# Loading each value row once, and copying the shared half tile on GpSimd, for the first four token tiles of a fused attention and two-MoE kernel

## The chip, the cores and the metric

The kernel runs on one core of one Trainium2 chip. Its time is the device time of one execution in microseconds (us). A core has five engines with an instruction queue each: PE (TensorE, matrix products), DVE (VectorE), ACT (ScalarE), POOL (GpSimd) and SP (SyncE, which here only starts transfers). The engines run side by side and wait for one another through semaphores; each takes its own instructions strictly in the order in which they stand. Transfers (DMA) from the chip's memory are cut into packets, which 16 DMA engines share.

## What is computed

Sliding-window attention over 4 sequences of 576 tokens with 8 heads of 64 values, then two feed-forward layers over all 2304 tokens. All inputs are f32.

```python
def _attn_ref(q, k, v):                     # (4, 8, 576, 64) each
    scores = scale * np.matmul(q, k.transpose(0, 1, 3, 2))
    mask = (rel >= 0) & (rel < window)      # rel = row - column, window = 64
    ...
    return np.matmul(attn, v)
...
h = x @ w_in                                # 512 x 2048
g = np.where(pos, h, np.where(neg, 0.0, (h + beta) ** 2 / (4.0 * beta)))
x = g @ w_out                               # 2048 x 512
...                                         # second layer: 512 x 1024, soft-max gate, layer norm, 1024 x 512
```

With a window of 64, a query looks at the 64 rows of its own range and at the 64 rows of the range ahead of it, and at no others.

## The kernel before

**Tiles.** Tokens go in 12 tiles of 192 (TT), three to a sequence. A tile has three ranges of 64 queries (QB). For each range i of tile t the kernel holds one value tile `vw[t, i]` of 128 rows by 8 heads by 64: rows 0 to 63 are the value rows of the preceding range, rows 64 to 127 those of the range itself. So the lower half of one value tile holds the same rows as the upper half of the one before it. `load_v(t)` (L294 to L303) fills the three tiles of t by three transfers from SP, each of 256 KB, in a ring of 6 buffers. For the first range of a sequence, which has nothing ahead of it, it loads only 64 rows, its own (128 KB), into the lower half, and the products there use 64 rows only (`first`, L341).

**Attention.** A group g is one tile and one pair of heads (4 groups to a tile). `st_qkt` puts queries and keys into shape, `st_s` makes the scores (PE into ps_s at L352, DVE L360 for mask and maximum, ACT L366 for the exponentials), `st_norm` divides by the sum (DVE L377 and L378, then L382 and L386 on POOL for the first three tiles and on DVE afterwards), `st_t` transposes the weights on PE (ps_p, L400 and L402, brought back by ACT L405 and L407), and `st_v` multiplies with the value tiles (ps_x, L421) and splits the result into a high and a low part (ACT L428 to xh, DVE L429 to xl).

**First layer.** Tokens go in 6 blocks of 384 (j). For each of 16 slices f of the hidden width, `moe_h` makes ps_h (L496, 12 matmuls), the gate is formed on ACT, DVE and POOL (L505, L506, u at L511, gh at L512, gl at L516; L516 is on POOL in block 0 and on DVE later), and `moe_y` adds into four accumulators (L527, 12 matmuls). In block 0 the slices f = 0 and 1 are done in two halves: first for the tokens of tile 0, then for those of tile 1. The numbers U0, U1, ... below count the L511 instructions: U0 and U1 are the two slices of tile 0, U2 and U3 those of tile 1, U4 is f = 2 for all 384 tokens.

**Weights.** The first layer's weights are loaded during block 0 and kept. Each of 32 units W0 to W31 (512 KB each, two for each slice f, alternating w_in and w_out) passes one conveyor: a transfer by SP into one of 5 staging buffers wst (L124 or L126), DVE L136, ACT L132, DVE L137, ACT L145 (the high part, wih or woh), POOL L146 (the low part, wil or wol). Only when POOL is through with a unit is its staging buffer free for the transfer of the unit five places later.

**What sets the order.** The source issues work in slots, but a scheduler orders each engine's instructions from the time it supposes that each takes. A change in one transfer therefore moves instructions on all engines. After block 0, PE goes through blocks 1 to 5 and the second layer.

## Time and profile before

| | us |
|---|---|
| median of 3 runs (lowest to highest) | 710.56 (709.49 to 712.19) |
| profiled execution | 712.67 |
| its span, first to last instruction | 710.9 |
| PE busy in the span | 685.6 |
| block 0, about | 0 to 130 |
| PE busy from 0 to 130 | 112.7 |
| PE busy from 130 to 432 (302 us) | 302.0 |

The profile counts from the first instruction; 1.8 us of the profiled execution lie around its span. A stretch is read by asking what the engine that sets the pace waited for in it. PE is busy without a break from 130 to 432, so of the first layer it is block 0 that holds PE's idle time. The granted TensorE clock is given as a share of 2.4 GHz, so 0.50 is the lower of its two levels, 1.2 GHz.

### The profile page before, as it was taken

To read this page: it belongs to the slowest core of one execution; us is meant where nothing else is said; L and a number is where in the kernel's file an instruction comes from. 1 tells how busy PE (TensorE), PEld (TensorE's weight loads), DVE (VectorE), ACT (ScalarE), POOL (GpSimd) and SP (SyncE) were. 2 spreads that over 40 slices of the span, in tenths; PEclk is the share of its full clock that TensorE was granted. 3 is DMA by queue.
4 is the path that set the end of the run, shared out by engine and by line. 5 is a ranking of instruction groups with operands and counts; after the bars stand their busy time and mean duration, and the time that the engine had idled before them with its cause. 6 is when DMAs were issued, how large, how long until landed. Compare 5 with 4: busy or idle time off the path is not lost.

```text
span 710.9 us, 12663 instructions
## 1 busy us (share of the span) xinstructions
PE 685.6 (96%) x4439; PEld 630.0 (89%) x4439; DVE 434.3 (61%) x1147; ACT 413.0 (58%) x1006; POOL 195.3 (27%) x217
## 2 busy tenths in 40 slices
PE   6899978999999999999999999999999899999998
PEld 5689768999999999999999999999988678888887
DVE  4549898555555555454455543642379799988850
ACT  5778886565566655565566665454455635545541
POOL 2358876200001000021112111652472223300000
PEclk9989999999999999999999999999999999999999
DMA  9986897534353623346352211452033554553321
GB/s 193 216 231 171 220 260 189 107 81 107 71 110 88 139 61 73 78 124 130 87 112 70 95 60 47 154 200 89 1 126 97 175 164 155 175 177 122 131 74 45
DMA packets 155544, 88.94 MB, mean 125 GB/s; under 512 B 118616, under 2 KB 141400, under 8 KB 155480
## 3 DMA queue, kind: packets, MB, share of 16 engines
q1 hardware_dynamic: 144040, 64.00, 36.4%
q0 software_dynamic: 8704, 19.41, 8.4%
q10 hardware_dynamic: 2736, 4.72, 1.8%
q8 instruction: 35, 0.57, 0.4%
q14 instruction: 29, 0.24, 0.1%
HBM read 63.97 MB, written 24.12 MB: 124 GB/s over the span
## 4 chain that ended last, share of the span: by engine, by line
PE 72%; DVE 10%; issue 7%; POOL 4%; DMA 3%; ACT 2%; SPq 1%; DVEq 0%; POOLq 0%; ACTq 0%
PE ps_h L496 22%; PE acc L527 22%; PE ps_o L826 13%; PE P L711 7%; PE ps_x L476 2%; PE ps_p L402 2%; PE ps_s L442 2%; PE ps_s L352 2%; DVE wst L137 2%; POOL wil L249 2%; DVE wst L136 1%; PE ps_x L421 1%; DMA wst<-in_moe_w_out_dram 1%; DVE gl L516 1%; DVE s L740 1%
## 5 line engine op out<-in xcount | busy, mean ns | idle before, releaser
L511 DVE SCALAR_TENSOR_TENSOR u<-u,ps_h 128x384 f32<-128x384 f32 (+1 forms) x98 | 53.2, 543 | 143.8 <-ACT u L506 140.2
L496 PE MATMUL ps_h<-xh,wih 128*128 128x384 f32 (+1 forms) x392 | 132.6, 339 | 3.2 <-DVE u L511 3.1
L496 PE MATMUL ps_h<-xl,wih 128*128 128x384 f32 (+1 forms) x392 | 131.5, 336 | 1.4 <-DVE xl L429 1.4
L527 PE MATMUL acc<-gl,woh 128*128 128x384 f32 (+1 forms) x392 | 130.7, 335 | 2.2 <-DVE gl L516 1.3
L496 PE MATMUL ps_h<-xh,wil 128*128 128x384 f32 (+1 forms) x392 | 131.5, 336 | 0.0
L527 PE MATMUL acc<-gh,wol 128*128 128x384 f32 (+1 forms) x392 | 129.7, 333 | 0.0
L527 PE MATMUL acc<-gh,woh 128*128 128x384 f32 (+1 forms) x392 | 126.9, 342 | 0.0
L505 ACT ACTIVATE u<-ps_h,half 128x384 f32<-128x384 f32 (+1 forms) x98 | 55.9, 572 | 92.6 <-PE ps_h L496 92.4
L512 ACT CAST gh<-u 128x384 fp32r<-128x384 f32 (+1 forms) x98 | 49.7, 507 | 55.0 <-DVE u L511 37.8
L496 PEld LDWEIGHTS ps_h<-xh,wih 128*128 128x128 f32 x392 | 74.6, 190 | 5.2 <-DVE u L511 4.7
L527 PEld LDWEIGHTS acc<-gl,woh 128*128 128x128 f32 x392 | 73.8, 188 | 3.5 <-DVE gl L516 1.7
L496 PEld LDWEIGHTS ps_h<-xl,wih 128*128 128x128 f32 x392 | 74.7, 190 | 2.2 <-DVE xl L429 2.0
L516 DVE TENSOR_TENSOR gl<-u,gh 128x384 fp32r<-128x384 f32 x80 | 52.8, 661 | 37.3 <-ACT gh L512 36.7
L527 PEld LDWEIGHTS acc<-gh,woh 128*128 128x128 f32 x392 | 72.4, 188 | 3.0 <-issue 2.4
L496 PEld LDWEIGHTS ps_h<-xh,wil 128*128 128x128 f32 x392 | 74.7, 190 | 0.1
L527 PEld LDWEIGHTS acc<-gh,wol 128*128 128x128 f32 x392 | 73.7, 188 | 0.0
L711 PE MATMUL P<-wih,x2p 128*128 128x512 f32 x216 | 70.6, 391 | 0.5 <-DVE xo L539 0.5
L826 PE MATMUL ps_o<-woh,wol 128*128 128x512 f32 (+1 forms) x152 | 58.6, 385 | 2.9 <-DVE wol L814 2.9
L826 PE MATMUL ps_o<-woh,woh 128*128 128x512 f32 (+1 forms) x152 | 58.4, 384 | 0.0
L826 PE MATMUL ps_o<-wol,woh 128*128 128x512 f32 (+1 forms) x152 | 58.0, 382 | 0.0
L506 ACT ACTIVATE u<-u 128x384 f32<-128x384 f32 (+1 forms) x98 | 51.0, 521 | 2.0
L711 PEld LDWEIGHTS P<-wih,x2p 128*128 128x128 f32 x216 | 40.5, 188 | 9.2 <-DVE xo L539 0.9
(125 smaller groups left out, 1250.8 us busy)
## 6 DMA issues: line engine op xcount, KB each, us to landing
vw<-in_v_dram SPq DMA_DIRECT2D x32, 256.0 KB, 5.2
wst<-in_moe_w_in_dram SPq DMA_DIRECT2D x16, 512.0 KB, 5.2
wst<-in_moe_w_out_dram SPq DMA_DIRECT2D x16, 512.0 KB, 5.5
lnd<-e SPq DMA_DIRECT2D x16, 512.0 KB, 2.7
lT<-lnd SPq DMA_DIRECT2D x64, 128.0 KB, 3.0
x2d<-xo POOLq DMA_DIRECT2D x24, 192.0 KB, 2.5
out_dram<-o ACTq DMA_DIRECT2D x17, 256.0 KB, 2.9
wst<-in_moe_w_in_dram POOLq DMA_DIRECT2D x8, 512.0 KB, 5.3
```

Of the source, the lines that this page charges most:

```text
L137: nc.vector.scalar_tensor_tensor(high, high, 3, low, op0=ALU.logical_shift_left, op1=ALU.bitwise_or)
L249: nc.gpsimd.tensor_tensor(lo, v_, as_f32(hi), op=ALU.subtract)
L352: nc.tensor.matmul(ps[:, i * 128 + c0:i * 128 + 128], qT[g][:, i, :, :].rearrange("p x q -> p (x q)"), kT[g][:, i * 64 + c0:i * 64 + 128], ...
L496: nc.tensor.matmul(ps, a, bb[:, kc, c], start=(n == 0), stop=(n == 3 * KC - 1))
L505: nc.scalar.activation(u, ps, ACTF.Relu, bias=half, scale=0.5)
L506: nc.scalar.activation(u, u, ACTF.Square)
L511: g = nc.vector.scalar_tensor_tensor(u, u, 1.0, ps, op0=ALU.min, op1=ALU.max)
L512: return nc.scalar.copy(hi, u).ins, g.ins
L516: eng.tensor_tensor(lo, u, as_f32(hi), op=ALU.subtract)
L527: nc.tensor.matmul(acc[j, e][:, c], a, bb, start=(f == 0 and n == 0 and c.start == 0), stop=(f == NF - 1 and n == 2),)
L711: nc.tensor.matmul(ps, l, r, start=(n == 0), stop=(n == 5))
L826: nc.tensor.matmul(ps, a[kk // 4][:, kk % 4, :], b[kk][:, c:c + w], start=(n == 0), stop=(n == 3 * NK2 - 1),)
```

## The change

For tiles t = 0 to 3 (NVC = 4), `load_v` loads only the 64 rows of the range itself, into the upper half of the value tile (128 KB), and GpSimd copies the upper half of the preceding value tile into the lower half. The first range of a sequence no longer has a tile of its own: it uses the lower half of the second range's tile, which is still loaded whole (`vw[t, 0] = vw[t, 1]`). From tile 4 on nothing is changed.

```diff
-    G0, F0, NC, NQ, NV = 6, 2, 4, 6, 7
+    G0, F0, NC, NQ, NV, NVC = 6, 2, 4, 6, 7, 4
...
         for i in range(QB):
-            w = at_p.tile([128, H, D], F32, tag="vw", bufs=6, name="vw")
             s0 = tl * TT + i * 64 - 64
+            if t < NVC and s0 < 0:
+                continue
+            w = vw[t, i] = at_p.tile([128, H, D], F32, tag="vw", bufs=6, name="vw")
             if s0 < 0:
                 nc.sync.dma_start(out=w[0:64], in_=v[b, :, 0:64, :].rearrange("h p d -> p h d"))
+            elif t < NVC and s0 > 0:
+                nc.sync.dma_start(out=w[64:128], in_=v[b, :, s0 + 64:s0 + 128, :].rearrange("h p d -> p h d"))
+                nc.gpsimd.tensor_copy(w[0:64], (vw[t, i - 1] if i else vw[t - 1, QB - 1])[64:128])
             else:
                 nc.sync.dma_start(out=w, in_=v[b, :, s0:s0 + 128, :].rearrange("h p d -> p h d"))
-            vw[t, i] = w
+        if t < NVC and tl == 0:
+            vw[t, 0] = vw[t, 1]
```

Lines behind L304 stand 6 further down in the changed kernel (L386 is L392 there, and so on). The copies are L305. There are 8 of them: one for tile 0, three each for tiles 1 and 2, one for tile 3; they are called C0 to C7 below.

**POOL, from the start to the normalization of group 2.** The names are p (softmax weights of a group), rs (reciprocal sums) and vw (value tiles). Before:

```order
L382 TENSOR_TENSOR p<-p,rs 128x64
L386 TENSOR_TENSOR p<-p,rs 128x256
L382 TENSOR_TENSOR p<-p,rs 128x64
L386 TENSOR_TENSOR p<-p,rs 128x256
L382 TENSOR_TENSOR p<-p,rs 128x64
```

Now, at the same place:

```order
L305 COPY vw<-vw 64x512
L388 TENSOR_TENSOR p<-p,rs 128x64
L392 TENSOR_TENSOR p<-p,rs 128x256
L305 COPY vw<-vw 64x512
L388 TENSOR_TENSOR p<-p,rs 128x64
L392 TENSOR_TENSOR p<-p,rs 128x256
L146 TENSOR_TENSOR wil_146<-wst,wih_145 128x512
```

C0 stands ahead of the first group's normalization and C1 ahead of the second's; W0's low part has moved ahead of group 2.

**PE, around the weight transposes of group 6 (the last ps_p here).** wih_168 and wil_169 before, and wih_170 and wil_171 now, are the two parts of unit W2, of the slice f = 1. Before:

```order
L402 MATMUL ps_p<-ident,p 128x128 x3
L421 MATMUL ps_x<-pT,vw 64x64 x6
L402 MATMUL ps_p<-ident,p 128x128 x3
L496 MATMUL ps_h<-xh,wih_168 128x192
L496 MATMUL ps_h<-xl,wih_168 128x192
```

Now:

```order
L502 MATMUL ps_h<-xl,wih_170 128x192
L502 MATMUL ps_h<-xh,wil_171 128x192
L502 MATMUL ps_h<-xh,wih_170 128x192
L502 MATMUL ps_h<-xl,wih_170 128x192
L502 MATMUL ps_h<-xh,wil_171 128x192
L427 MATMUL ps_x<-pT,vw 64x64 x7
L408 MATMUL ps_p<-ident,p 128x128 x3
L427 MATMUL ps_x<-pT,vw 64x64 x5
```

All of slice f = 1 for tile 0 now stands ahead of group 6's transposes; before, it stood behind them.

**POOL, from unit W4 (wil_177 before, wil_179 now) on.** Before:

```order
L146 TENSOR_TENSOR wil_177<-wst,wih_176 128x512
L516 TENSOR_TENSOR gl<-u,gh 128x192
L386 TENSOR_TENSOR p<-p,rs 128x384
L516 TENSOR_TENSOR gl<-u,gh 128x192
L146 TENSOR_TENSOR wol_364<-wst,woh_363 128x512
L146 TENSOR_TENSOR wil_412<-wst,wih_411 128x512
L386 TENSOR_TENSOR p<-p,rs 128x384
L516 TENSOR_TENSOR gl<-u,gh 128x192
L386 TENSOR_TENSOR p<-p,rs 128x384
L516 TENSOR_TENSOR gl<-u,gh 128x192
L146 TENSOR_TENSOR wol_461<-wst,woh_460 128x512
```

Now, from the second copy of tile 2 (C6) to U2's gl:

```order
L305 COPY vw<-vw 64x512
L146 TENSOR_TENSOR wil_414<-wst,wih_413 128x512
L392 TENSOR_TENSOR p<-p,rs 128x384
L146 TENSOR_TENSOR wol_463<-wst,woh_462 128x512
L146 TENSOR_TENSOR wil_500<-wst,wih_499 128x512
L146 TENSOR_TENSOR wol_524<-wst,woh_523 128x512
L392 TENSOR_TENSOR p<-p,rs 128x384
L146 TENSOR_TENSOR wil_533<-wst,wih_532 128x512
L305 COPY vw<-vw 64x512
L146 TENSOR_TENSOR wol_625<-wst,woh_624 128x512
L146 TENSOR_TENSOR wil_629<-wst,wih_628 128x512
L522 TENSOR_TENSOR gl<-u,gh 128x192
```

Six more units (W7 to W12, wol_463 to wil_629) are ahead of U2's gl than before, where W7 (wol_461) stood behind U3's. DVE's order has moved in the same way: W7 to W12 stand ahead of U2, and U4 behind W15, where before W10 was the last unit ahead of U4.

## Rows read from the trace of the kernel before

**Rows 1.** Stretches: length, busy us of each engine (instructions), PEclk, DMA share, GB/s.
```profile
0.00:130.00 130.00, 112.69 (x770) 100.79 (x771) 95.16 (x266) 96.98 (x275) 78.28 (x78) 0.97 0.85 204
130.00:432.00 302.00, 302.00 (x2341) 291.96 (x2341) 155.42 (x505) 181.45 (x484) 37.06 (x54) 1.00 0.40 93
```

**Rows 2.** Stretches between 80 and 130 us, same columns.
```profile
80.00:90.00 10.00, 8.65 (x58) 7.27 (x56) 8.04 (x10) 6.79 (x14) 10.00 (x8) 1.00 0.78 187
90.00:100.00 10.00, 7.52 (x43) 6.82 (x44) 9.64 (x24) 8.35 (x20) 6.31 (x6) 1.00 1.01 254
100.00:110.00 10.00, 7.94 (x53) 6.96 (x52) 9.66 (x23) 7.52 (x21) 7.62 (x7) 1.00 1.07 269
```

**Rows 3.** Stretches between 34 and 80 us, same columns.
```profile
34.00:42.00 8.00, 6.85 (x48) 6.39 (x48) 3.07 (x13) 5.42 (x17) 6.67 (x6) 0.57 1.07 262
42.00:80.00 38.00, 36.32 (x284) 33.98 (x279) 33.00 (x80) 33.41 (x88) 25.80 (x22) 1.00 0.72 204
36.00:38.00 2.00, 2.00 (x19) 1.71 (x17) 0.17 (x1) 1.73 (x5) 2.00 (x2) 0.50 0.97 320
```

**Rows 4.** Timeline: start, length, engine, line; in brackets idle before it, and releaser.
```profile
12.86 0.42 PE L400 MATMUL ps_p<-ident,p 128*64 128x128 f32 x1
...
35.15 0.90 PE L402 MATMUL ps_p<-ident,p 128*128 128x128 f32 x3 [1.45 <-POOL p L386]
...
51.57 0.35 DVE L511 SCALAR_TENSOR_TENSOR u<-u,ps_h 128x192 f32<-128x192 f32 x1 [1.70 <-ACT u L506]
```

**Rows 5.** Timeline of POOL, same columns.
```profile
10.25 0.61 POOL L386 TENSOR_TENSOR p<-p,rs 128x256 f32<-128x256 f32 x1
...
29.00 0.83 POOL L386 TENSOR_TENSOR p<-p,rs 128x384 f32<-128x384 f32 x1 [6.84 <-DVE rs L378]
31.77 0.83 POOL L386 TENSOR_TENSOR p<-p,rs 128x384 f32<-128x384 f32 x1 [1.94 <-ACT p L366]
34.01 1.09 POOL L386 TENSOR_TENSOR p<-p,rs 128x384 f32<-128x384 f32 x1 [1.41 <-DVE rs L378]
35.06 1.75 POOL L146 TENSOR_TENSOR wil<-wst,wih 128x512 fp32r<-128x512 f32 x1
...
44.26 0.60 POOL L516 TENSOR_TENSOR gl<-u,gh 128x192 fp32r<-128x192 f32 x1 [2.24 <-ACT gh L512]
```

**Rows 6.** DMA of 12 to 30 us, SP's queue: packets, MB, share of 16 engines.
```profile
q1 hardware_dynamic: 11034, 4.46, 122.7%
```

**Rows 7.** Timeline of SP's queue, and transfers to landing: wst (0 to 130 us), vw (0 to 12 us).
```profile
4.80 0.72 SPq L300 DMA_DIRECT2D vw<-in_v_dram  x1
...
33.41 0.36 SPq L126 DMA_DIRECT2D wst<-in_moe_w_out_dram  x1
...
DMA to landing us min/median/max: 3.7/5.3/8.0
...
vw<-in_v_dram SPq DMA_DIRECT2D x2, 256.0 KB, 4.7
```

**Rows 8.** Waits of 0 to 30 us (PE's for transfers): total us, times, longest.
```profile
PE ps_t L334 <- DMA qkn<-in_q_dram: 4.1, 3, 2.7
```

**Rows 9.** Groups by form, DVE of 0 to 130 us, and of 130 to 450 us: count, busy us, mean ns.
```profile
L137 DVE SCALAR_TENSOR_TENSOR wst<-wst 128x512 uint32<-128x512 uint32 x32 | 34.4, 1081 | 2.5 <-ACT wst L132 2.2
L136 DVE TENSOR_SCALAR wst<-wst 128x512 uint32<-128x512 uint32 x32 | 22.7, 711 | 2.4 <-DMA wst<-in_moe_w_out_dram 2.4
...
L137 DVE SCALAR_TENSOR_TENSOR wst<-wst 128x512 uint32<-128x512 uint32 x16 | 11.0, 690 | 0.4
L136 DVE TENSOR_SCALAR wst<-wst 128x512 uint32<-128x512 uint32 x16 | 6.8, 422 | 0.0
```

**Rows 10.** Groups by form, ACT and POOL of 0 to 130 us.
```profile
L132 ACT ACTIVATE wst<-wst 128x512 f32<-128x512 f32 x32 | 21.7, 681 | 1.0 <-DMA wst<-in_moe_w_in_dram 0.7
L145 ACT CAST wih<-wst 128x512 fp32r<-128x512 f32 x16 | 10.6, 662 | 4.0 <-DVE wst L137 3.9
...
L146 POOL TENSOR_TENSOR wil<-wst,wih 128x512 fp32r<-128x512 f32 x16 | 23.5, 1470 | 1.8 <-ACT wih L145 1.8
```

## The prediction

> **What bounds the kernel now.** I read the stretches first. From 130 us on PE is busy without a break, 302.0 us of 302, and before that 112.69 of 130 us [rows 1]. So time is lost or won in block 0, and what is won there moves everything behind it: the question is how much PE idle time the change removes or adds there. Then I looked for where that idle time lies. About 5 us are the start. One piece lies at 34 us: PE waits 1.45 us for POOL's normalization of group 6 [rows 4], and behind it the granted clock falls to 0.50; over 34 to 42 us it is 0.57 on average, and from 42 us on it is full [rows 3]. The other piece lies between 80 and 110 us: 1.35 + 2.48 + 2.06 = 5.9 us [rows 2]. There DVE is busy 9.6 of 10 us in two of three stretches and POOL all of the first, so it is the conveyor of the weights that PE waits on.
>
> Next, what the transfers hold up. They are dense from the start, 122.7% of the 16 engines by packet time between 12 and 30 us (packets overlap, so it can pass 100%) [rows 6]. But the waits of the first 30 us end on a transfer only for the first queries, 4.1 us in three waits, all ahead of the value loads [rows 8]. No engine waits there for a value tile or a weight. So the volume that the change removes is not what PE waits for directly, and its worth is indirect: it lets SP come earlier to the next weight transfers, and it made the scheduler put the instructions into another order.
>
> Last, the prices on the conveyor. DVE's L137 takes 1081 ns on average in block 0 and 690 ns later, L136 711 and 422 ns, for the same tiles [rows 9]. What differs is that POOL is busy 78.28 of the first 130 us and 37.06 of the following 302 [rows 1]. I take it that DVE is slowed by POOL's work beside it; of the copies this touches only those that fall beside L136 and L137, in the conveyor. The Trainium skill, GPSIMD Engine Reference, section 8, says that GpSimd shares its SBUF interfaces with VectorE, and names instructions with two SBUF inputs and those in a 2-port mode; the rows agree, and the rule speaks against the change: by it alone all 8 copies could hold up DVE for their whole length, 8 x 0.9 = 7.2 us at the price taken below, and the sum would end at +4 instead of -2.4.
>
> **The change part by part.**
>
> *Transfers removed.* Eight transfers shrink from 256 to 128 KB and two of 128 KB vanish: 8 x 128 + 2 x 128 = 1280 KB, in rows of 64 x 4 = 256 bytes, so 5120 packets. One packet of this mix took 1.227 x 16 x 18 us / 11034 = 32 ns, so 5120 of them are 10.2 us of all 16 engines; by bytes (4.46 MB in 18 us, 248 GB/s) 5.3 us [rows 6]. Half of it, 640 KB of tiles 0 and 1, lies ahead of the transfer of W5, which SP issued at 33.41 us [rows 7]; one half tile of tile 2 (128 KB) is moved ahead of it. W5 can so be issued 512 KB earlier, 2.1 us by bytes to 4.1 us by packets. On the path this is nothing by itself (no wait ends there); it is the condition for the terms below.
>
> *Copies added, at the start.* C0 stands ahead of group 0's normalization and must wait for the first value tile: issued at 4.80, 4.7 us to landing, so 9.5 us [rows 7]. No row shows a copy. The nearest are a two-input product of 256 columns, 0.61 us, and L146 with two inputs and 512 columns, 1.47 us on average [rows 5, 10]; I take 0.9 for 512 columns and one input, nearer the longer row in size and half of it in inputs. The Trainium skill, GPSIMD Engine Reference, section 4.1, says that an operation with one input runs at about line rate; with the 1.2 GHz of its section 1 I make of that an estimate of 0.43 us for 512 columns. By that estimate all eight copies would hold POOL for 3.4 us instead of the 7.2 that I use, and the sum below would be 0.2 us lower. With 0.9 us C0 ends at 10.4 and the normalization, due at 10.0 and ending at 10.86, ends at 11.3; PE takes its transposes at 12.86 [rows 4, 5]. So C0 costs nothing, with 1.5 us in reserve. C1 follows it with the same reserve, and C2 to C4 stand ahead of group 4's normalization, where POOL waits 6.84 us until 29.00 [rows 5]. C5 to C7 stand in the conveyor, ahead of low parts of W4, W6 and W11; there POOL has waits like that of 2.24 us ahead of 44.26 [rows 5]. Cover gone, they cost 3 x 0.9 = 2.7 us of POOL, with 1.3 us each 3.9. Below zero they can't go, since nothing leaves POOL. I take +0.5.
>
> *PE at 34 us.* In the new order the transposes of group 6 stand behind slice f = 1 of tile 0, so that PE need not wait for POOL with nothing to do; W2's low part on POOL has moved ahead of group 6's normalization. If PE is fed without a gap, 1.45 us go, and with them the slow clock: 8 us at 0.57 are 8 x 0.43 = 3.4 us of PE's work [rows 3]; together -4.9. The other end is zero: slice f = 1 needs W2's low part, which POOL can begin at 31.77 + 0.83 = 32.6 at the earliest and ends 1.5 us later, 34.1, so the gap may only change its cause [rows 5, 10]. I take half, -2.4.
>
> *The conveyor moved forward.* DVE is idle for 8 - 3.07 = 4.9 us of 34 to 42 us [rows 3]. In the new order W7 to W12 stand ahead of U2, before W6 was the last. If DVE fills its idle time with them, the last units are done earlier and PE's 5.9 us between 80 and 110 go [rows 2]. That is one end, -5.9; the other is 0, if the conveyor is held by the five buffers instead. I take -2.5, rather less than half, since DVE's work is the same and it is busy 33.00 of the 38 us that follow [rows 3].
>
> *A wait added: U2 behind W12.* U2 now stands behind W12 on DVE, and PE can't go far without it, as the two banks for ps_h are taken. W12 can be loaded only when POOL is through with W7, and W7 only when it is through with W2. W2 ended on POOL at 35.06 + 1.75 = 36.8. W7 then takes a landing of 5.3, L136 0.42, L132 0.68, L137 0.69, L145 0.66 and L146 1.47 = 9.2 us, to 46.0; W12 lands at 51.3 and is through L136, L132 and L137 at 53.1. U2 stood at 51.57: +1.5 us [rows 4, 5, 7, 9, 10]. With landings of 8.0 and block 0's means on DVE (0.71, 1.08) W7 takes 12.6 us, to 49.4, and W12 is through at 49.4 + 8.0 + 2.5 = 59.9: +8.3 us. With W2 ahead of group 6's normalization it is 1.1 us less. I take +2.0, near the short end, since POOL is not yet full there. Queued behind W12 on DVE are U2, U3 and the scores of the next groups; PE waits for them.
>
> *The sum:* 0.5 - 2.4 - 2.5 + 2.0 = -2.4 us. The profiled execution, 712.67 us (span 710.9 and 1.8 around it), would become 710.3; it lay 2.1 above the median of the runs, 710.56, so for the median I forecast 708.2.
>
> **The rivals.** *Feeding wins on all counts.* The gap at 34 us and the 5.9 us at 80 to 110 go nearly whole and U2 comes in time: -4.9 - 5.9 + 1.5 = -9.3 at most, 701.3. I give it as 701 to 705. For it speaks that DVE and the transfers both get room; against it that DVE and POOL are nearly full between 80 and 110 us [rows 2]. *The wait behind W12 wins.* DVE, in order, stands at W12, later at W15 ahead of U4, for weights that the five buffers hold back, and PE, idle for only 1.7 of the 38 us between 42 and 80 now [rows 3], runs dry. It decides from where one landing with its conversion takes over 11 us instead of 9.2. At its long end +8.3, with the gains halved -2.4, +0.5 for copies: +6.4, 717.0; as a range 712.5 to 718. *Nothing comes of it.* The gap stays with another cause, the conveyor is paced by DVE and POOL as before, and the copies hide: 709.7 to 712.
>
> **How the numbers follow.** A measurement of this kernel can tell about 0.5% from no change, here 3.6 us: faster is under 707.0, slower over 714.1. My forecast (705 to 709.7) has a chance of 0.42, of which 0.17 lies under 707.0; the full gain 0.20, all of it faster; the wait behind W12 0.23, of which 0.18 lies over 714.1; nothing 0.15. So faster 0.37, same 0.25 + 0.05 + 0.15 = 0.45, slower 0.18. The range leaves out the lowest part of the full gain and the upper part of the rival, together under 2 in 10: 701.5 to 715.5.
>
> **What would show it.** Right: POOL's copies at 0.6 to 1.3 us; SP's transfer of W5 at 29 to 31 us instead of 33.41; no PE gap over 1 us and no clock of 0.50 between 30 and 42 us; the value tiles with 5120 packets fewer; PE idle between 80 and 110 under 4 us. Wrong: U2 after 54 us with DVE or ACT waiting for a wst transfer ahead of it; POOL waiting at C5, C6 or C7 for a landing; PE idle between 42 and 80 us for well over 1.7 us. If copies take much over 1.3 us, or slow DVE's L137 beyond 1081 ns, the copies' term is wrong; if the last unit leaves POOL as late as before while PE is idle less early on, the conveyor term is.

## The result, and the profile of the changed kernel

| | before | changed |
|---|---|---|
| median of 6 runs each, us | 710.02 | 718.28 |
| lowest to highest | 708.75 to 712.19 | 715.80 to 724.09 |
| ratio of the two, 95% interval | | 1.0113 (1.0081 to 1.0145) |
| profiled execution, span | 712.67, 710.9 | 716.50, 714.7 |

The change makes the kernel slower by 1.1%, 8 us. The two profiled executions lie 3.8 us apart: that of the changed kernel is near its shortest runs, that of before is 2.65 us above its median in this table. To keep the part that the change touches apart from the end of the program I use a mark: the 61st U step, in the stretch where PE is busy without a break. First the row of before, then that of the changed kernel (timeline of DVE; L511 of before is L517 now, and every line from L310 on has moved by 6).

```profile
342.93 0.56 DVE L511 SCALAR_TENSOR_TENSOR u<-u,ps_h 128x384 f32<-128x384 f32 x1 [1.08 <-ACT u L506]
```
```profile
348.94 0.56 DVE L517 SCALAR_TENSOR_TENSOR u<-u,ps_h 128x384 f32<-128x384 f32 x1 [1.08 <-ACT u L512]
```

So 6.0 us are lost ahead of the mark, which I call **U60**. Behind it before takes 710.9 - 342.9 = 368.0 us and the changed kernel 365.8. There PE, DVE, ACT and POOL have the same work in the same order in both; that difference is taken up with e18. The mark of one execution is good to about 1 us: before, e10, e12 and e18, which are the same up to there, lie up to 0.9 us apart at 28 us already.

Where the 6.0 us are shows in two long stretches, before and then changed. The columns are those of [rows 1]: length, busy us of PE, PEld, DVE, ACT and POOL, PEclk, DMA share, GB/s.

```profile
30.00:80.00 50.00, 45.94 (x353) 42.37 (x353) 39.52 (x108) 42.80 (x118) 33.30 (x28) 0.93 0.76 204
80.00:140.00 60.00, 52.98 (x349) 48.19 (x348) 48.45 (x114) 41.93 (x111) 38.70 (x32) 1.00 0.78 183
```
```profile
30.00:80.00 50.00, 41.60 (x292) 37.51 (x291) 40.89 (x96) 42.31 (x112) 40.35 (x34) 0.83 0.72 199
80.00:140.00 60.00, 55.69 (x367) 51.86 (x367) 42.03 (x108) 39.33 (x106) 30.21 (x26) 0.97 0.70 169
```

Between 30 and 80 us PE is idle for 8.4 us instead of 4.1, and the granted clock is 0.83 on average instead of 0.93. Counted in pieces of 2 us (idle time, plus busy time x (1 - clock)), PE lost 7.1 us there before and 15.9 now: +8.8. Between 80 and 140 us, where the prediction hoped for a gain, it lost 7.0 before and 6.0 now: -1.1. In steps of 10 us the changed kernel reads:

```profile
30.00:40.00 10.00, 8.80 (x57) 7.34 (x56) 5.24 (x12) 9.05 (x26) 8.04 (x9) 0.66 0.92 214
40.00:50.00 10.00, 7.66 (x79) 6.83 (x78) 8.69 (x18) 7.50 (x19) 7.36 (x7) 1.00 0.74 247
50.00:60.00 10.00, 8.49 (x50) 7.56 (x51) 9.95 (x27) 9.56 (x31) 7.98 (x7) 0.66 0.87 236
60.00:70.00 10.00, 7.44 (x64) 6.91 (x63) 9.67 (x20) 7.69 (x17) 8.13 (x8) 1.00 0.68 207
70.00:80.00 10.00, 9.21 (x48) 8.86 (x48) 7.34 (x22) 8.52 (x22) 8.84 (x7) 0.83 0.40 90
80.00:90.00 10.00, 10.00 (x70) 9.56 (x69) 5.21 (x16) 5.92 (x17) 4.67 (x5) 1.00 0.64 193
...
100.00:110.00 10.00, 8.12 (x55) 6.84 (x54) 9.38 (x23) 8.27 (x22) 6.63 (x5) 1.00 0.97 237
110.00:120.00 10.00, 8.04 (x53) 7.08 (x51) 9.79 (x20) 6.90 (x19) 7.79 (x8) 1.00 0.82 200
```

Read the DVE column: DVE is nearly full from 40 to 70 us and half idle at 80 to 90. In the kernel before it filled up later (stretches of before):

```profile
40.00:50.00 10.00, 9.48 (x91) 8.79 (x90) 5.25 (x19) 7.21 (x24) 4.68 (x5) 0.92 0.71 202
50.00:60.00 10.00, 9.74 (x80) 9.45 (x81) 8.40 (x20) 9.73 (x27) 5.76 (x6) 1.00 0.62 161
```

The new order does the conversions of weights early, and PE runs dry early. What PE waits for between 40 and 78 us (waits: total us, times, longest):

```profile
PE ps_x L427 <- ACT p L372: 1.7, 1, 1.7
PE ps_h L502 <- DVE u L517: 1.6, 2, 0.8
PE ps_t L340 <- DVE mx L366: 1.6, 1, 1.6
```

And what stands on DVE ahead of these (timeline of DVE): conversions, then the scores of a group, then U2, at 56.90 instead of 51.57 [rows 4].

```profile
50.68 1.15 DVE L137 SCALAR_TENSOR_TENSOR wst<-wst 128x512 uint32<-128x512 uint32 x1
51.75 0.42 DVE L136 TENSOR_SCALAR wst<-wst 128x512 uint32<-128x512 uint32 x1
...
53.22 3.02 DVE L137 SCALAR_TENSOR_TENSOR wst<-wst 128x512 uint32<-128x512 uint32 x2
56.27 0.29 DVE L366 CUSTOM_DVE_ANT_0 p<-ps_s,mask 128x128 f32<-128x128 f32 x1
...
56.90 0.35 DVE L517 SCALAR_TENSOR_TENSOR u<-u,ps_h 128x192 f32<-128x192 f32 x1
```

The copies themselves are small (timeline and group of POOL; the first and the seventh copy): the first, C0, waits for its transfer, as foreseen, and ends at 10.36; no later one waits. Most take 0.60 to 0.62 us, two 0.95, and all eight 5.4 us.

```profile
9.76 0.60 POOL L305 COPY vw<-vw 64x512 f32<-64x512 f32 x1 [7.04 <-DMA vw<-in_v_dram]
...
41.02 0.95 POOL L305 COPY vw<-vw 64x512 f32<-64x512 f32 x1
...
L305 POOL COPY vw<-vw 64x512 f32<-64x512 f32 x8 | 5.4, 695 | 7.4 <-DMA vw<-in_v_dram 7.0
```

### The profile page after: what moved, and what is told of

Read it like the earlier page. It is cut to its first block, busy times and chain, and to the rows that moved or that the text cites. A ratio compares the mean times of both kernels' runs of the same rounds, so it can differ in the third digit from the quotient of the medians.

```text
span 714.7 us, 12675 instructions
## 1 busy us (share of the span) xinstructions
PE 688.4 (96%) x4439; PEld 634.3 (89%) x4439; DVE 433.8 (61%) x1147; ACT 413.5 (58%) x1006; POOL 199.0 (28%) x225
## 4 chain that ended last, share of the span: by engine, by line
PE 70%; DVE 9%; DMA 6%; issue 6%; SPq 4%; POOL 3%; ACT 2%; DVEq 0%; POOLq 0%; ACTq 0%
PE acc L533 23%; PE ps_h L502 22%; PE ps_o L832 12%; PE P L717 7%; SPq L279 2%; DVE wst L137 2%; PE ps_x L482 2%; DMA wst<-in_moe_w_in_dram 2%; PE ps_s L448 2%; DMA wst<-in_moe_w_out_dram 2%; DVE wst L136 2%; POOL wil L249 2%; PE ps_p L408 1%; DVE gl L522 1%; DMA x2r<-x2d 1%
## 5 line engine op out<-in xcount | busy, mean ns | idle before, releaser
L517 DVE SCALAR_TENSOR_TENSOR u<-u,ps_h 128x384 f32<-128x384 f32 (+1 forms) x98 | 53.3, 544 | 149.2 <-ACT u L512 146.7
L533 PE MATMUL acc<-gh,woh 128*128 128x384 f32 (+1 forms) x392 | 130.7, 344 | 0.0
L511 ACT ACTIVATE u<-ps_h,half 128x384 f32<-128x384 f32 (+1 forms) x98 | 56.0, 573 | 96.2 <-PE ps_h L502 95.9
L518 ACT CAST gh<-u 128x384 fp32r<-128x384 f32 (+1 forms) x98 | 49.6, 506 | 54.1 <-DVE u L517 36.5
```

What stands on the lines that cost most here:

```text
L511: nc.scalar.activation(u, ps, ACTF.Relu, bias=half, scale=0.5)
L517: g = nc.vector.scalar_tensor_tensor(u, u, 1.0, ps, op0=ALU.min, op1=ALU.max)
L518: return nc.scalar.copy(hi, u).ins, g.ins
L533: nc.tensor.matmul(acc[j, e][:, c], a, bb, start=(f == 0 and n == 0 and c.start == 0), stop=(f == NF - 1 and n == 2),)
```

## The experiments

The theory that I started from: not the copies and not the half loads cost the time, but the other order into which the scheduler put the instructions. To test it I wrote an order down. Each kernel traces its instructions in the order of the program text; a table gives, for each engine, the numbers of its first instructions (up to about 140 us) in the order wanted, and each is tied behind the one ahead of it, in issue order only:

```python
def pin_order(tc):
    by = {}
    for i in tc.nc.cur_bb.bb.instructions:
        ...
        by.setdefault(str(i.engine).split(".")[-1], []).append(i)
    for e, runs in PINS.items():
        ...
        for a, b in zip(order, order[1:]):
            tc.add_manual_dep(by[e][b], by[e][a].name,
                mybir.DependencyInfo(mybir.DependencyClass.NoSync, mybir.DependencyReason.DATA),
                ...
```

**e1: the old work in the new order.** The kernel before, with the table of the changed kernel (the stretch of DVE's shown holds the last conversions ahead of U2, W10 to W12, then U2 and U3).

```diff
+PINS = {
+    "DVE": (
...
+        "75-77 97 99 84 78-80 102 100 103 87-89 92 107 101 98 108 94-95 93 113 116 114 117 119 109 120 124 "
...
+    pin_order(tc)
```

> The loads of before (12 for the first four tiles, every row of a shared half loaded twice, no copy on GpSimd), but the order of the changed kernel on all five engines up to about 140 us (PE, VectorE, ScalarE word for word; one load of a later tile stands where the ring of six allows it). Theory 'order': the loss comes from the new order of the instructions, so this kernel loses as the changed one does, 715 to 721 us against 710.0. Rival 'copies and half loads': the work itself costs the time, so without it the time is that of before, 709 to 712. If both share it: 713 to 715.

Measured: 719.26 us (718.63 to 721.00), ratio 1.0105 (1.0068 to 1.0142). The order alone brings the whole loss, without a copy and without a half load.

**e2: the new work in the old order.** The changed kernel with the table of before, each copy ahead of the POOL instruction that follows it in the changed kernel.

```diff
+PINS = {
+    "DVE": (
...
+        "45-48 42 49 59 50 57 61 53-54 60 62 55 71 63-65 58 67-68 72 66 83 69-70 73-77 79-80 84 78 92 81 "
...
+    pin_order(tc)
```

> The mirror: the half loads and the eight copies of the changed kernel, in the order of before on all five engines (each copy stands ahead of the instruction of GpSimd that follows it in the changed kernel). Theory 'order': 708 to 711.5 us, at most the 1 to 2 us better that 640 KB fewer bytes ahead of the first weights might give; U2 starts at 51 to 52 us. Rival 'copies and half loads': 715 to 720 us.

Measured: 712.65 us (710.87 to 714.64), ratio 1.0011 (0.9992 to 1.0029): no difference that can be told from the kernel before, which stood at 711.54 in that round, though 1.2 us above the range expected. The mark says the same, for e1 and then e2 (timeline of DVE):

```profile
353.77 0.56 DVE L586 SCALAR_TENSOR_TENSOR u<-u,ps_h 128x384 f32<-128x384 f32 x1 [1.08 <-ACT u L581]
```
```profile
343.00 0.56 DVE L595 SCALAR_TENSOR_TENSOR u<-u,ps_h 128x384 f32<-128x384 f32 x1 [1.08 <-ACT u L590]
```

Half loads and copies together are worth 343.00 - 342.93 = 0.1 us in the old order, which is nothing within the 1 us that a mark can tell, and the new order costs 10.8 us with the old loads. (This execution is the slowest of e1's four; in the time, e1 and the changed kernel lose the same.) No run pins a kernel's own order and does nothing else, but e10 and e18 below, pinned to the old order, are no slower than before, and e4, pinned to the new one but for a piece on SP, is as slow as the changed kernel. So the first question is settled: it is the order. The next is which part of it.

**e3: the old order, but the new one on SP.**

```diff
     "SP": (
-        "0-21 24-27 47-54 22-23 29-31 28 32-34 37 35 38 36 39-41 55-63 42 64-65 43 66-68 44 69-71 45 72-73 46 "
...
+        "0-21 24-27 29 47-51 22 52-54 23 30-31 28 32-39 103 40-46 55-92 95-100 93 101-102 94 104-106 109-111 "
...
```

> The changed kernel's loads and copies, the order of before on PE, VectorE, ScalarE and GpSimd, and the changed kernel's order on SP, which issues the transfers. It tells which half of the order counts. If the engines' order (weight conversions ahead of U2, U4, U5 on VectorE) is what costs: 708 to 712 us. If the order of the transfers is (24 query loads ahead of W21): 714 to 720 us, with PE idle for several us between 80 and 110 us.

Measured: 719.64 us, ratio 1.0113 (1.0082 to 1.0145). But the loss has a cause that the changed kernel does not have (timeline of DVE): in the old order DVE comes to group 12 before SP, in the new order, has loaded its queries.

```profile
82.49 0.78 DVE L408 STREAM_TRANSPOSE kq<-qk 64x192 f32<-64x192 f32 x2 [7.24 <-DMA qk<-in_q_dram]
```

So e3 tells only that the orders of two engines can't be exchanged one by one. It does not tell the halves apart.

**e4: W21 to W24 ahead of 24 query loads.** In the changed kernel DVE waits 3.79 us for the transfer of W21, which SP starts at 83.77 us behind 24 query loads (timelines of SP and DVE):

```profile
80.92 2.75 SPq L291 DMA_DIRECT2D qk<-in_k_dram  x4
83.77 0.39 SPq L126 DMA_DIRECT2D wst<-in_moe_w_out_dram  x1
```
```profile
87.84 0.43 DVE L136 TENSOR_SCALAR wst<-wst 128x512 uint32<-128x512 uint32 x1 [3.79 <-DMA wst<-in_moe_w_out_dram]
```

```diff
-        "0-21 24-27 29 47-51 22 52-54 23 30-31 28 32-39 103 40-46 55-92 95-100 93 101-102 94 104-106 109-111 "
+        "0-21 24-27 29 47-51 22 52-54 23 30-31 28 32-39 103 40-46 79-82 55-78 83-92 95-100 93 101-102 94 "
```

> The changed kernel with one thing moved: on SP the transfers of W21 to W24 stand ahead of the 24 query loads that follow W20, all else as it is. If the second half of the loss is that the conveyor's lead of 9 to 11 us at W20 is thrown away there: W21 is converted by 80 us instead of 90, PE is idle under 1 us between 100 and 120 us instead of 3.8, and the time falls by 3 to 6 us to 712 to 715. If the dry spells of PE between 40 and 80 us and their low clock are all of the loss: 716 to 719, unchanged.

Measured: 719.93 us, ratio 1.0114 (1.0081 to 1.0148): nothing won. DVE now waits for the queries instead (timeline of DVE), and POOL takes up W21's low part at 91.6 us as against 90.0.

```profile
85.16 0.78 DVE L406 STREAM_TRANSPOSE kq<-qk 64x192 f32<-64x192 f32 x2 [4.54 <-DMA qk<-in_q_dram]
```

**e5 and e6: only the order of conversions and U steps on DVE.** e5 is the changed kernel, left to the scheduler but for one chain on DVE, in which L136, L137 and L517 stand among themselves as before; e6 is the kernel before with the chain of the changed one.

```diff
+PINS = {
+    "DVE": (
+        "43-44 51-52 56 59 57 61 60 62 71 83 69-70 73-74 92 81 101 82 85 90 86 96 91 97 109 99 118 100 "
...
```

> The changed kernel's loads and copies, ordered by the scheduler, with one thing fixed: among the conversions of weights (L136, L137) and the U steps on VectorE the order is that of before, so that W6 and not W12 is the last conversion ahead of U2. Theory 'conversions ahead of U': it is this that empties PE between 40 and 76 us, so the time comes back to 708 to 712.5, and PE is idle and slow together for 6 to 9 us between 30 and 80 us (7.1 before, 15.9 changed). Rival 'the rest of the order' (PE's own order, the grouping of the attention steps): the time stays at 715 to 720.

> The mirror: the kernel before, ordered by the scheduler, with only the order among conversions and U steps on VectorE fixed to that of the changed kernel (W12 ahead of U2, W13 ahead of U3, W20 ahead of U5). Theory 'conversions ahead of U': 715 to 722 us, with 13 us or more of idle and slow time of PE between 30 and 80 us. Rival 'the rest of the order': 709 to 713.

Measured: e5 716.27 us, ratio 1.0086 (1.0052 to 1.0119); e6 728.50 us, ratio 1.0242 (1.0208 to 1.0276). The stretches of e5 and then e6:

```profile
30.00:80.00 50.00, 45.30 (x341) 41.16 (x340) 35.52 (x87) 38.45 (x103) 33.27 (x30) 0.92 0.70 190
80.00:140.00 60.00, 53.61 (x321) 49.52 (x319) 48.85 (x116) 41.73 (x110) 36.64 (x29) 0.91 0.67 167
```
```profile
30.00:80.00 50.00, 37.84 (x286) 34.20 (x284) 38.59 (x104) 39.40 (x110) 31.98 (x27) 0.76 0.75 196
80.00:140.00 60.00, 50.53 (x312) 47.32 (x311) 44.38 (x97) 39.87 (x96) 34.85 (x29) 0.94 0.67 172
```

In e5 PE's loss between 30 and 80 us is nearly gone, as expected (8.2 us; the changed kernel had 15.9, before 7.1). But the time comes back by 2 us only, not to the 708 to 712.5 expected, since 80 to 140 us now holds 10.9 us of loss instead of 6.0. In e6 the chain makes the kernel before slower than the range given, most of it between 30 and 80 us (20.2 us). That points to the conversions ahead of the U steps on DVE as one cause of the early loss. It does not isolate them: in both kernels the scheduler reorders all the rest around the chain, and in e5 it gives the gain away later.

**e7 and e8: the change for one tile, and for two.**

```diff
-    G0, F0, NC, NQ, NV, NVC = 6, 2, 4, 6, 7, 4
+    G0, F0, NC, NQ, NV, NVC = 6, 2, 4, 6, 7, 1
```

> The change made for the first token tile alone (NVC = 1: one copy, 256 KB of loads less), ordered freely. W8 is then the last conversion ahead of U2 (W6 before, W12 with all four tiles). Theory 'conversions ahead of U': between the two and near before, 709 to 713 us. Rival 'each removed load gains by itself': 706 to 709. Rival 'any new order of block 0 loses': 715 to 720.

> The change made for the first two token tiles (NVC = 2), ordered freely; W11 is the last conversion ahead of U2. Theory 'conversions ahead of U': nearly the loss of the whole change, 714 to 719 us. Rival 'the rest of the order' or 'any new order loses' can't be told from it here; rival 'the last tiles' copies or loads cost' (C5 to C7, tile 3): 709 to 712.

Measured: NVC = 1 712.68 us, ratio 1.0023 (0.9995 to 1.0050); NVC = 2 714.05 us, ratio 1.0051 (1.0028 to 1.0073). With 0, 1, 2 and 4 tiles the last unit converted ahead of U2 is W6, W7 (with the first step of W8), W11 and W12, PE's loss between 30 and 80 us is 7.1, 8.1, 14.1 and 15.9 us, and the ratio 1, 1.002 (which can't be told from 1), 1.005 and 1.011: the fewer bytes ahead of the weights, the further the scheduler pulls conversions forward, and the more PE loses early. In the runs without extra products on PE the two go together throughout: 7.1 to 9.3 us where U2 stands behind W6 or W7, 14.1 to 20.5 us where it stands behind W10 to W12.

**e9 and e10: six conversions halved.** Both in their own order, new and old; the other halves of these weights stay unconverted.

```diff
     def split_b(st, *_):
         low, high = st[:, :, 0], st[:, :, 1]
+        n_split.append(0)
+        if 8 <= len(n_split) <= 13:
+            low, high = st[:, 0:256, 0], st[:, 0:256, 1]
```

> The changed kernel in its own order on all engines, with L136 and L137 of W7 to W12 done on half of their columns (the other halves of these six weights stay unconverted). That takes some 0.8 us off VectorE for each, about 5 us in all, and in this order all of it between 45 and 60 us. Theory 'VectorE, filled with conversions, keeps the attention steps and U2 waiting there': idle and slow time of PE between 30 and 80 us falls from 15.9 to 8 to 11 us, and the time to 711 to 714 us. Rival 'PE's own order leaves it nothing to do there, whatever VectorE does': 716 to 719.

> The control for the run before: the kernel before in its own order with the same six conversions halved (W7 to W12 lie between 55 and 70 us there). VectorE has 1.7 us of idle time and PE 0.9 us in that stretch, so little is to be won: 707.5 to 710.5 us by the theory on VectorE and by its rival alike; below 706 would say that any us off VectorE is worth as much in the old order as in the new.

Measured: e9 717.29 us, ratio 1.0079 (1.0050 to 1.0108); e10 709.64 us, ratio 0.9982 (0.9961 to 1.0002). U60 comes 1.8 us earlier than in the changed kernel in e9 and 1.0 earlier than before in e10. But 0.4 and 0.6 of these stand ahead of the first halved conversion already, so halving won about 1.4 us in the new order and 0.4 in the old. On DVE L136 and L137 of W7 to W12 took 7.0 us instead of 11.4 in e9, and 8.3 instead of 10.6 in e10. And PE's loss between 30 and 80 us (16.7 us) did not fall: my number for e9 was wrong.

**e11: PE kept busy in the new order.** 29 products with weights of zero ahead of seven waits of PE.

```diff
+    def warm(o, n, start=False):
+        for _ in range(n):
+            nc.tensor.matmul(o[0:64, 0:128], ident[0:64, 64:128], ident[0:64, :], start=start, stop=start)
...
+                if j == 0 and c == FIRST:
+                    warm(ps, {(0, 10): 5}.get((f, n), 0))
...
+            if j == 0 and e == 0:
+                warm(acc[0, 0], {(1, 0): 12, (1, 192): 9, (2, 0): 3}.get((f, c.start), 0))
```

> The changed kernel in its own order, with 29 extra products of PE (64 rows, 128 columns, weights zero, added to an open accumulation, so nothing in the output changes) put ahead of the seven instructions at which PE waits 0.7 to 1.7 us between 31 and 76 us. They lengthen no wait; they fill it. Theory 'the granted clock falls to 0.50 because of these waits': one or two of the three falls between 30 and 80 us are gone, the slow time there drops from 7.5 to 4 us or less, and the time is 714 to 716.5. Rival 'the clock falls for another reason': three falls, 718 to 721 us.

Measured: 717.68 us, ratio 1.0096 (1.0072 to 1.0120), between the two ranges given. Of three low stretches of the clock between 30 and 80 us one is left (PEclk 0.93 over the stretch, 0.83 without the products), and yet U60 comes at 352.6, 3.7 us later (0.8 of them ahead of the first product): U2 is at 57.6 as against 56.9. The products took what the waits and the slow clock had taken. In the new order PE's low clock is a consequence: PE waits for DVE there, at either level.

```profile
30.00:80.00 50.00, 45.16 (x348) 39.89 (x349) 41.67 (x91) 42.32 (x113) 40.45 (x33) 0.93 0.72 198
```

**e12: PE kept busy in the old order.** The kernel before in its own order, ten such products at the waits of 31 and 34 us.

```diff
+                if j == 0 and c == FIRST:
+                    warm(ps, {(0, 7): 4}.get((f, n), 0))
...
+        if g in {6: 6}:
+            warm(ps, {6: 6}[g], True)
```

> The kernel before in its own order, with 10 such products of zero: 4 at the wait of 0.84 us at 31 us, 6 at the wait of 1.45 us at 34 us, behind which the granted clock is 0.50 for 7 us. Theory 'the clock falls because of these waits': no clock of 0.50 between 30 and 42 us, up to 3.1 us won, 707 to 709.5 us, which would beat both kernels. Rival: the fall stays, 710 to 712 us.

Measured: 705.67 us (705.00 to 707.62), ratio 0.9932 (0.9907 to 0.9956): it beats both kernels, by more than expected. The wait for POOL's normalization is 0.44 us where [rows 4] had 1.45, and the clock does not fall behind it: 1.00 over 34 to 42 us instead of 0.57 [rows 3] (timeline of PE, then the stretch).

```profile
32.74 1.52 PE L569 MATMUL ps_p<-ident 64*64 64x128 f32 x12
34.70 0.55 PE L482 MATMUL ps_p<-ident,p 128*128 128x128 f32 x3 [0.44 <-POOL p L464]
```
```profile
34.00:42.00 8.00, 7.56 (x81) 6.99 (x80) 5.37 (x18) 7.60 (x24) 6.66 (x7) 1.00 1.13 280
```

U60 comes at 340.08, 2.9 us earlier. Of these about 0.9 stand at 28 us already, ahead of the first product, so the filled waits are worth about 2 us there. That is not the whole gain; the last experiment tells the rest.

**e13 and e17: the new work in the old order, PE kept busy, and one copy moved.** e13 is e2 with the products of e12. e17 moves one copy on POOL (number 29, C5) behind W5's low part.

```diff
     "Pool": (
-        "12 16-17 13 18-21 26 22-23 31 14-15 28 24-25 27 32-33 29 35 37 34 42 36 30 39 38 46 44 49 41 43 45 "
+        "12 16-17 13 18-21 26 22-23 31 14-15 28 24-25 27 32-33 35 37 34 42 36 29-30 39 38 46 44 49 41 43 45 "
```

> The changed kernel's loads and copies in the order of before, with the 10 products of zero at the two waits near 31 and 34 us that made the kernel before faster (705.7 us). If half loads and copies are worth nothing either way: 704.5 to 707.5 us. If the 640 KB fewer bytes gain once the clock no longer hides it: 701 to 704. If the copies cost: 708 to 712.

> The run before (new loads and copies, old order, PE's two waits filled) with one copy moved on GpSimd: the one that waited at 39.45 us for its transfer stands behind W5's low part instead of ahead of W4's. Theory 'a copy that waits for its transfer holds up GpSimd's queue, and PE behind it': U2 comes at 48 to 49 us instead of 52.6, no low clock at 42 to 47 us, 704.5 to 707 us. Rival 'the loads or the other copies cost': 708.5 to 711.

Measured: e13 710.18 us, ratio 0.9985 (0.9964 to 1.0006); e17 707.20 us, ratio 0.9948 (0.9931 to 0.9966). In e13 (timelines of POOL and PE) C5 waits 1.79 us, until the transfer that it copies from has landed (at 39.30 us) as far as the trace lets one say; the bracket names PE, in e2 at the same place the transfer. Behind it stand W4's low part, U's low parts and a normalization; PE then waits 2.70 us.

```profile
39.45 0.61 POOL L383 COPY vw<-vw 64x512 f32<-64x512 f32 x1 [1.79 <-PE ps_t L418]
...
42.81 1.01 POOL L470 TENSOR_TENSOR p<-p,rs 128x384 f32<-128x384 f32 x1
```
```profile
42.90 0.36 PE L619 MATMUL acc<-gl,woh 128*128 128x192 f32 x1 [2.70 <-POOL gl L608]
```

With that copy moved, U60 comes at 342.1 instead of 344.6, and the time falls by 3.0 us, to 0.2 above the range given. In e2 the same copy waits at the same place (39.21 us, 1.39 us for its transfer) and costs nothing: PE is at its slow clock then and comes late anyway. In the old order the cover of the copy was the slow clock. Without it the new work still costs something: at the mark e17 is 2.0 us behind e12, of which 0.8 stand at 28 us already.

**e14, e15 and e16: two repairs of the new order.** e14 moves conversions W5 to W18 back behind attention and U steps on DVE, ACT and POOL, e15 interleaves W21 to W24 with the query loads on SP, e16 does both. Of e14 a stretch on DVE, of e15 the line of SP:

```diff
-        "75-77 97 99 84 78-80 102 100 103 87-89 92 107 101 98 108 94-95 93 113 116 114 117 119 109 120 124 "
+        "84 78-80 96-97 87-89 99 92 102 100 103 101 98 94-95 93 107-108 113 109 104-106 132-134 111-112 115 "
...
-        "0-21 24-27 29 47-51 22 52-54 23 30-31 28 32-39 103 40-46 55-92 95-100 93 101-102 94 104-106 109-111 "
+        "0-21 24-27 29 47-51 22 52-54 23 30-31 28 32-39 103 40-46 79 55-62 80 63-70 81 71-78 82-92 95-100 93 "
```

> The changed kernel in its own order, except that on VectorE, ScalarE and GpSimd the steps of the conversions W5 to W18 may stand less far ahead of the attention and U steps of groups 7 to 11 (their places in the program text differ by at most 80 instead of some 150 numbers; PE and SP unchanged). Theory 'attention and U queued behind conversions': norms of groups 8 to 10 come 3 to 6 us earlier than 52.8, 60.6 and 73.8 us, and the time falls to 712 to 716. Rival 'the queue of transfers behind W20 alone': 717 to 720.

> The changed kernel in its own order, with one thing moved on SP: behind W20 the transfers stand as W21, eight query loads, W22, eight, W23, eight, W24, instead of 24 query loads and then W21 to W24. Theory 'weights and queries hold each other up in SP's queue': VectorE waits neither 3.8 us for W21 nor 4.5 us for queries, W21 leaves GpSimd by 84 us instead of 90, and the time falls by 2 to 4 us to 714 to 716.5. Rival 'what PE lost before 80 us is all': 717 to 720.

> Both edits, attention first and interleaved transfers. If both theories hold and add up: 709 to 713 us. If one of them is all: its time, 712 to 716. If neither: 717 to 720.

Measured: e14 731.95 us, ratio 1.0277 (1.0223 to 1.0331); e15 718.95 us, 1.0103 (1.0063 to 1.0144); e16 723.93 us, 1.0183 (1.0146 to 1.0221). All three expectations fell. In e15 SP starts W21 at 71.65 us and DVE waits for no transfer there, but now for PE (timeline of DVE), and POOL takes up W21's low part at 89.5 us.

```profile
81.38 0.29 DVE L442 CUSTOM_DVE_ANT_0 p<-ps_s,mask 128x128 f32<-128x128 f32 x1 [2.59 <-PE ps_s L434]
```

In e14 the attention steps did not come earlier as a whole: the reciprocals of groups 8 and 9 stand at 54.1 and 63.4 us, behind the changed kernel's 52.8 and 60.7, and only that of group 10 is ahead. The loss shows at the other engines: PE waits 7.0 us for the low parts of U (L596) on POOL, which stand behind low parts of weights that come late now. Each queue of the new order fits the others; moving a piece of one or three of them only moved the wait.

**e18: a control for e12.** The ten products of zero in one place at 67 us, where PE has work queued.

```diff
+            if j == 0 and e == 0:
+                warm(acc[0, 0], {(2, 0): 10}.get((f, c.start), 0))
```

> The kernel before in its own order, with ten products of zero as in e12, but all in one place near 60 us, where PE has work queued. Theory 'it is the filled wait that keeps the clock': the fall at 34 to 41 us stays, and the products cost what they take, 0 to 2.6 us: 710.5 to 713.5 us. Rival 'any added work of this kind keeps the clock up': 705 to 708.

Measured: 707.60 us (706.06 to 709.61), ratio 0.9949 (0.9931 to 0.9966): the rival's time, though not for its reason. The clock falls at 34 us as before (0.57 over 34 to 42 us), and U60 comes at 342.16, 0.8 us earlier than before. That is not the products' doing. U2, 16 us ahead of them, is 0.7 us early already (50.91 us instead of 51.57): from 14 us on PE was faster for a while in this execution, as the same transpose of before and then e18 shows (timelines of PE). The views give the clock of both stretches as 1.00, so the lengths have to be read.

```profile
15.48 0.42 PE L400 MATMUL ps_p<-ident,p 128*64 128x128 f32 x1
```
```profile
14.84 0.27 PE L479 MATMUL ps_p<-ident,p 128*64 128x128 f32 x1
```

The gain is behind U60, where 363.3 us pass instead of 368.0. These are the stretches of before, then e18:

```profile
550.00:570.00 20.00, 17.14 (x75) 13.57 (x74) 14.42 (x31) 12.78 (x25) 4.27 (x7) 1.00 0.50 159
570.00:590.00 20.00, 20.00 (x83) 16.34 (x82) 17.41 (x39) 10.28 (x19) 5.92 (x6) 0.91 0.44 145
```
```profile
550.00:570.00 20.00, 20.00 (x88) 16.08 (x87) 16.93 (x37) 12.18 (x24) 4.48 (x7) 1.00 0.52 184
570.00:590.00 20.00, 20.00 (x90) 16.57 (x89) 18.63 (x43) 10.36 (x19) 4.86 (x6) 1.00 0.48 160
```

Before waits 2.9 us in the second layer (waits of PE, 430 us to the end), and the clock falls behind that; e18 does not, though the work of PE, DVE, ACT and POOL stands in the same order.

```profile
PE ps_o L826 <- DVE wol L814: 2.9, 2, 2.2
```

The wait goes back to a transfer: DVE waits for POOL there, and POOL for x2r (timeline of POOL). In before SP starts x2r at 559.19 us, behind four transfers (lT) that start 3.74 us after the one ahead of them (lnd); in e18 these start 2.69 us after it, x2r is started 1.9 us earlier, counted from U60, and POOL waits 8.23 us.

```profile
564.70 1.46 POOL L680 TENSOR_TENSOR xs<-x2r 128x256 f32<-128x256 f32 x2 [10.42 <-DMA x2r<-x2d]
```

So of e12's 7.1 us of span 2.9 lie ahead of U60, where the control has 0.8; with what stood ahead of the products taken off, these are about 2 and 0.2. The other 4.3 lie behind U60, come with the control's products as well, and so are not the filled waits' doing. In the time e12 and e18 can't be told apart, as their intervals overlap; the clock at 34 us and the mark tell them apart. All runs, by the mark:

| kernel | ratio to before | U60 at | behind U60 |
|---|---|---|---|
| before | 1 | 342.9 | 368.0 |
| changed | 1.0113 | 348.9 | 365.8 |
| e1 old loads, new order | 1.0105 | 353.8 | 365.4 |
| e2 new loads, old order | 1.0011 | 343.0 | 368.4 |
| e3 | 1.0113 | 349.4 | 368.3 |
| e4 | 1.0114 | 350.8 | 366.8 |
| e5 | 1.0086 | 346.3 | 368.0 |
| e6 | 1.0242 | 358.4 | 369.2 |
| e7, e8 (1 and 2 tiles) | 1.0023, 1.0051 | 342.4, 348.5 | 365.8, 364.9 |
| e9, e10 | 1.0079, 0.9982 | 347.1, 342.0 | 365.0, 368.3 |
| e11 | 1.0096 | 352.6 | 364.2 |
| e12 old order, waits filled | 0.9932 | 340.1 | 363.7 |
| e13, e17 | 0.9985, 0.9948 | 344.6, 342.1 | 364.0, 363.7 |
| e14, e15, e16 | 1.0277, 1.0103, 1.0183 | 362.3, 352.0, 356.6 | 367.7, 368.5, 366.1 |
| e18 | 0.9949 | 342.2 | 363.3 |

## Why the prediction was wrong, step by step

**What bounds the kernel** was read rightly in the main: the time was decided in block 0, and no wait of PE ended on a value tile. But that PE waited for the conveyor between 80 and 110 us was concluded from DVE's and POOL's busy shares. The waits themselves (PE in before, 80 to 110 us) are for DVE's normalization and U steps, so the conveyor was in the way there as work on DVE, not as weights that came late.

```profile
PE ps_p L400 <- DVE p L382: 2.8, 2, 1.7
PE ps_h L496 <- DVE u L511: 2.7, 4, 1.3
```

**The transfers** went as worked out: 5152 packets fewer in all, of which 5120 were counted, and SP started W5's transfer at 30.53 us, within the 29 to 31 given.

**The copies** cost about nothing in the old order (e2: 0.1 us at U60, 0.5 taken). One alone takes 0.60 us, not 0.9. The Trainium skill, GPSIMD Engine Reference, section 4.1, says about line rate for one input, which with the clock of its section 1 gave an estimate of 0.43 us, from the columns alone; the trace does not agree with that estimate, it has 0.60. That the copies hold up DVE for their whole length, which would have cost 7.2 us, falls with e2 as well: in the old order DVE's L137 took 1127 ns on average up to 130 us with the copies (e2) and 1069 to 1111 without them (before, e12, e18). The rule of the Trainium skill, GPSIMD Engine Reference, section 8, on the interfaces that GpSimd shares with VectorE, may bear on all these means, but no run shows a price of the copies by it. The price with the cover gone, 2.7 to 3.9 us for three copies, was met in size by luck: in e13 against e17 one copy, C5, cost 2.5 us at U60 (3.0 us in the time), by the wait for its landing and not by its own 0.6 us. And the cover in the old order was not the wait of POOL that the text named; it was PE's slow clock.

**PE at 34 us**, -2.4 taken, gave nothing: PE waits 1.06 us for DVE at 32.97 us, with the clock at 0.66 between 30 and 40 us. That was the end named as "the gap may only change its cause". In the old order, where e12 filled that wait and the one before it, about 2 of the 4.9 us given as the other end came out at U60.

**The conveyor moved forward**, -2.5 taken, gave 1.1. It did move: POOL took up W20's low part at 78.59 us instead of 89.27, and W31's still 4.9 us earlier. PE's idle time between 80 and 110 us fell from 5.9 to 1.9 us, under the 4 named as a sign. But behind the 3.79 us for which DVE waits for W21, PE was idle for 2.0 us between 110 and 120, where before it had no idle time, and the clock fell once more at 122 us (1.7 us). The step that failed here is that the lead of the conveyor lasts to its end and is PE's gain.

**U2 behind W12**, +2.0 taken, is the term that decided, and it was mis-sized. U2 came 5.3 us late, inside the range given, +1.5 to +8.3. But I priced it by landings and buffers, and chose the short end because POOL was not yet full. No conversion waited for a transfer there; DVE itself was full, 9.95 of 10 us between 50 and 60. And the sentence on what is queued behind W12, "the scores of the next groups", had no price: the reciprocals of groups 8, 9 and 10 came 3.6, 5.8 and 7.5 us late, and PE lost 8.8 us more between 30 and 80 us than before (half of it idle time, half low clock). Which of these late steps cost PE the time is not shown: in e6 the reciprocals came as early as before, U2 16 us late, and PE lost 20.2 us; in e9 both came 2 to 3 us earlier than in the changed kernel, and PE's loss did not fall. With the measured values the sum is 0 + 0 - 1.1 + 8.8 = +7.7. The mark has 6.0 and the medians 8.3; the 1.7 us between sum and mark are not accounted for.

So the rival "the wait behind W12 wins" came true, with 718.3 just past its upper end of 718; its place was right, its cause half right: DVE did stand at W12 ahead of U2, but not for weights that the five buffers held back. The chance of 0.23 was too low and the upper bound of 715.5 too near, because the order had not been priced as a whole: by 58 us the conveyor was four units further than before (W12 on POOL at 58.07 us, as against W8 at 58.46), some 4 x (1028 + 638 ns) = 6.7 us of DVE's time for L137 and L136, and I counted that as a gain and not as a delay of what it passed.

**What stays open.** The order is shown to be the cause (e1, e2). That conversions ahead of U on DVE are a part of it is made likely by e5 and e6 and by how closely the early loss follows them over all runs, for the stretch up to 80 us; it is not isolated. Which piece, put back alone, would bring back the time is not known: e4, e9, e11, e14 and e15 each took one suspect away and won at most 1 us; e5 won 2.

## What to carry to other kernels

Where a scheduler sets the order, price the new order and not only the edit: write out what each engine's queue now does first, and ask what it passes, since an in-order engine that fills its idle time with early work delays everything that becomes ready meanwhile. A kernel whose order is good can be kept so by pinning it (e2 against the changed kernel: 712.7 and 718.3 us with the same work). And a wait of PE can cost more than its length, by the low clock behind it; look at the granted clock there, and try to fill the wait, with a control that does the same work elsewhere (at the mark e12 gained about 2 us over its control, in the time the two can't be told apart).

## What the runs showed of the hardware that was not expected

A wait of 1.45 us and one of 0.84 us, filled with products of zero, kept the granted clock at its higher level through a stretch that ran at 0.57 on average without them (e12), while the same products 30 us later left the low clock where it was (e18). Whether a low clock costs anything depends on who is late: in the new order filling the waits raised the clock and won nothing (e11).

Executions differ at the start: in before the transpose at 15.5 us takes 0.42 us, in e18 at 14.8 us 0.27, and by 28 us e18 is 0.6 us ahead. A difference of that size at a mark is not the edit's.

Behind U60 the work of PE, DVE, ACT and POOL stands in one order in all 20 kernels. It takes 364.9 to 369.2 us in the 15 without the products and 363.3 to 364.2 in the five with them, wherever in block 0 they are. Each of the 15 has a wait of PE for DVE in the second layer, of 1.3 to 3.3 us, and none of the five; in before it goes back to the start of the transfer x2r. Why extra products between 30 and 75 us move that start was not tried and is open; of the 4.6 us by which e12 beats before, I would therefore call only the 2 us that it has over the control at U60 understood.
